# Half of the value copies of a two-layer attention kernel issued from GpSimd's queue instead of SyncE's

## The chip, the cores and the metric

The kernel runs on one core of one Trainium2 chip. The metric is the device time of one execution in microseconds (us); a measurement is the median of several runs. The profile shows one execution, taken by the hardware profiler. In it PE is TensorE (PEld its weight loads), DVE is VectorE, ACT is ScalarE, POOL is GpSimd and SP is SyncE; a "q" behind a name is that engine's instruction queue.

## The reference, cut to what matters

Four residual layers run one after the other over x of 2048 positions by 512 features, bf16: A, B, A, B. Both kinds have 32 heads of 16 features.

```python
def _A_ref(x, wqkv, w_phi, wo):        # linear attention over all positions
    ...
    phi_q = concatenate([softmax(q @ w_phi), softmax(-(q @ w_phi))])   # phi_k likewise
    kv = einsum("bhsf,bhsd->bhfd", phi_k, v);  z = phi_k summed over s
    o = (phi_q @ kv) / (phi_q @ z + 1e-6)
    return o @ wo
def _B_ref(x, wqkv, wo):               # each position sees 8 positions: 0, 2, ..., 14 behind it
    W, dil = 8, 2
    idx = pos[:, None] - (arange(W) * dil)[None, :]
    logits = einsum("bhsd,bhswd->bhsw", q, k[idx]) * Dh ** -0.5     # masked where idx < 0
    return einsum("bhsw,bhswd->bhsd", softmax(logits), v[idx]) @ wo
x = x + _A_ref(_layernorm(x), ...);  x = x + _B_ref(_layernorm(x), ...)
x = x + _A_ref(_layernorm(x), ...);  x = x + _B_ref(_layernorm(x), ...)
```

## The kernel before

The positions are cut into four blocks of 512 (b = 0 to 3); L = 0 or 1 counts the pairs of layers. "Block 12" means L = 1, b = 2. Every piece of work is a step of a named thread, and the string `_ORDER` (lines 57 to 97), written out in full, gives the one order in which all steps are issued. Each engine's queue holds its instructions in that order and runs them strictly one after the other, so an instruction that waits holds up all that stand behind it in the same queue. The buffers are given out by fixed tables (`_SLOTS`); a buffer's next user waits until the last reader is done. A DMA issue waits also for the landing of an earlier DMA that used the same one of eight completion semaphores of its queue.

The steps of a B layer for one block:

- `tr` (line 451, SyncE): a DMA transpose brings the normalised block xn to xnT. It waits for xn.
- `s_b1` (`mm`, line 927, TensorE): the projections to Q, K and V with the weights WB; `ev` copies each result from PSUM (lines 190 and 192, by VectorE or ScalarE). K and V have 16 columns of the block before at their left edge. GpSimd writes these edges with small copies: `halo` for K (line 953), `vhalo_out` (line 969) saves the tail of V and `vhalo_in` (line 965) puts it at the edge of the next block's V.
- `vrep(dl)` (lines 975 to 988), for dl = 0 to 3: four DMAs, one for each g in the order 0, 2, 1, 3, copy 32 rows of V of 4,208 bytes each, shifted by 2g columns, to the partitions 32g to 32g + 31 of a tile Vg. That is 131.5 KB for one DMA, 16 DMAs for a block and 128 for the kernel. "Copies 12.3" below are the four DMAs with dl = 3 of block 12.
- `s_b2` (`prod`, line 1019, VectorE): Q times K at eight shifts, a product of 4096 elements in each partition, four times a block. It reads K's edge. `lgt` (line 1026, TensorE) sums the products to logits, then come exponent, denominator (`den`, line 1042) and the weights PT.
- `s_b3` (`pav`, line 1081, VectorE): PT times Vg, one for each dl; it waits for the four copies of its dl. `mo` (line 1090, TensorE) sums, `ev` copies to oT, and `s_out` (line 520, TensorE, then line 533 on VectorE or 530 on ScalarE) multiplies by WoB and adds the residual.

Where the copies of values stand among the others: before the change all are in SyncE's queue, with the transposes `tr` between them. In `_ORDER` the GpSimd steps and the copies come in this order (tail is `vhalo_out`, V edge is `vhalo_in`, K edge is `halo`):

```
V00 tail | copies 00.0 | V01 edge, K01 edge, V01 tail | copies 01.0 | (tr) | K02 edge, V02 edge |
copies 01.1 01.2 01.3 | (tr, block 03) | copies 00.1 00.2 00.3 02.0 02.1 02.2 | K03 edge, V02 tail, V03 edge |
(tr) | copies 02.3 | (tr) | copies 03.0 03.1 03.2 03.3 | ... layer A ... |
copies 10.0 10.1 | K11 edge | (tr) | V10 tail | copies 10.2 10.3 | V11 edge, K12 edge | (tr) | copies 11.0 |
K13 edge | copies 11.1 11.2 11.3 | V11 tail, V12 edge, V12 tail, V13 edge |
copies 12.0 13.0 13.1 13.2 13.3 12.1 12.2 12.3 | stores of the result
```

The blocks' pavs come in the order 01, 00, 02, 03 in layer 0 and 10, 11, 13, 12 in layer 1; the last pav of blocks 12 and 13 is split in two halves.

Of the kernel before, what the change touches and what calls it, by code (L numbers as in the profile page):

```python
# [30 lines left out]
VGW = 3 * KVW + TB + 8  # L31
# [98 lines left out]
class _Fast:  # L130
# [788 lines left out]
    def s_b1(self, L, b):  # L919
        nc, add = self.nc, self.step  # L920
        st = "b1_%d%d" % (L, b)
        T = {}
        def mm(i, c):
            xnT = self.xnT["B%d" % L, b]
            T[i, c] = pp = self.ps()
            for k in range(NB):
                nc.tensor.matmul(pp[:], lhsT=self.WB[:, k, i * D + c:(i + 1) * D:NB], rhs=xnT[:, :, k, :],  # L927
                                 start=(k == 0), stop=(k == NB - 1))

        def ev(i, c, dve):  # L930
            if i == 0:
                if (L, b) not in self.QT:
                    self.QT[L, b] = self.med([NB, TB], "QT")
                dst = self.QT[L, b][:, c, :]
            elif i == 1:
                ktile()
                dst = self.K[L, b][:, c, 16:KVW]
            else:
                vtile()
                dst = T["V"][:, c, 16:KVW]  # L940
            self.copy(dve, dst, T[i, c][:])

        def ktile():
            if (L, b) not in self.K:
                self.K[L, b] = self.med([NB, KVW], "K")

        def vtile():
            if "V" not in T:
                T["V"] = self.med([NB, KVW], "V")

        def halo():
            ktile()
            nc.gpsimd.tensor_copy(out=self.K[L, b][:, :, 0:16], in_=self.K[L, b - 1][:, :, TB:KVW])

        def kzero():
            ktile()
            nc.gpsimd.memset(self.K[L, b][:, :, 0:16], 0.0)

        def vzero():
            vtile()  # L960
            nc.gpsimd.memset(T["V"][:, :, 0:16], 0.0)

        def vhalo_in():
            vtile()
            nc.gpsimd.tensor_copy(out=T["V"][:, :, 0:16], in_=self.vh[L, b - 1][:])

        def vhalo_out():
            self.vh[L, b] = self.sm([NB, 16], "vh", BF16)
            nc.gpsimd.tensor_copy(out=self.vh[L, b][:], in_=T["V"][:, :, TB:KVW])

        def vwr():
            self.VD[L, b] = self.dram.tile([P, NB * KVW], BF16, name="vd%d%d" % (L, b))
            nc.sync.dma_start(out=self.VD[L, b][:], in_=T["V"][:].rearrange("p c t -> p (c t)"))

        def vrep(dl):
            if dl == 0:
                self.Vg[L, b] = {}
            if dl % 2 == 0:
                self.Vg[L, b][dl // 2] = self.big([2, NB * KVW], "Vg")
            if (L, b) in _OPT["v_dram"]:  # L980
                a = self.VD[L, b][dl:dl + 1, 2:3]
                src = bass.AP(a.tensor, a.offset, [[2, 4], [4 * NB * KVW, H], [1, VGW]])
                nc.sync.dma_start(out=self.Vg[L, b][dl // 2][:, dl % 2, 0:VGW], in_=src)
                return
            for g in (0, 2, 1, 3):
                a = T["V"][dl:dl + 1, 0:1, 2 + 2 * g:3 + 2 * g]
                src = bass.AP(a.tensor, a.offset, [[4 * a.ap[0][0], H], [1, VGW]])
                nc.sync.dma_start(out=self.Vg[L, b][dl // 2][32 * g:32 * g + 32, dl % 2, 0:VGW], in_=src)

        if b:  # L990
            add(st + "v", "POOL", vhalo_in)
        else:
            add(st + "k", "POOL", kzero)
            add(st + "v", "POOL", vzero)
        for i in range(3):
            for c in range(NB):
                add(st + "qkv"[i], "PE", mm, i, c)
                self.flex(st + "qkv"[i], ev, i, c)
        if b:
            add(st + "kh", "POOL", halo)  # L1000
        if b < 3:
            add(st + "v", "POOL", vhalo_out)
        if (L, b) in _OPT["v_dram"]:
            add(st + "v", "SP", vwr)
        for dl in range(4):
            add(st + "v", "SP", vrep, dl)
# [232 lines left out]
class _Layout:  # L1239
# [6 lines left out]
    def add(self, name, nelem, nbuf=1):  # L1246
        self.regions[name] = (self.off, nelem, nbuf)
        self.off += nelem * nbuf
        return self
# [568 lines left out]
```

## Time and profile before

| what | value |
|---|---|
| median of 3 runs | 330.01 us (329.47 to 330.12) |
| span of the profiled execution | 327.5 us, first to last instruction |
| time around the span | 2.5 us, by the median (the profiled execution's own whole time is not recorded) |
| TensorE busy | 310.3 us, 95% |
| VectorE busy | 302.2 us, 92% |
| ScalarE busy | 279.3 us, 85% |
| GpSimd busy | 25.3 us, 8% |
| packets of SyncE's DMA queue | 34.81 MB, 53.6% of the 16 engines' span |
| mean granted TensorE clock | 0.998 |

A busy share is a mean over stages with different limits; the stage tells what a change in it is worth. In a row of a timeline stand the start, the time taken, the engine, the line, the operation, what it writes and reads, the shapes and the count; the brackets give the idle time before it and what ended that. DMA-issuing instructions of SyncE are not counted as busy; a DMA's time "to landing" runs from the start of its issue.

### The profile page before, as it was taken

How to read it: one execution, taken by the hardware profiler on the slowest of the kernel's cores; microseconds unless marked ns; L12 is line 12 of the kernel's file. 1: busy time of each engine (PE TensorE's matmuls, PEld its weight loads, DVE VectorE, ACT ScalarE, POOL GpSimd, SP SyncE). 2: the span in 40 equal slices, each digit the busy share in tenths (PEclk: the TensorE clock that was granted, in tenths of full speed). 3: DMA queues.
4: the chain of work that ended last, by engine and by line, in shares of the span. 5: the costliest groups of instructions: out<-in, count | busy, mean ns of one | idle time of the engine just before them, and what ended most of it. 6: DMA issues, size and time to landing. Idle time of an engine off the chain costs nothing. (4 is left out here: it accounts for less than half of the span.)

```text
span 327.5 us, 8033 instructions
## 1 busy us (share of the span) xinstructions
PE 310.3 (95%) x3176; PEld 149.5 (46%) x3203; DVE 302.2 (92%) x439; ACT 279.3 (85%) x634; POOL 25.3 (8%) x50
## 2 busy tenths in 40 slices
PE   7999999999999999999999999979999999999873
PEld 3655456445444444443444455644544454433221
DVE  7998995998998999899999999699999999999993
ACT  5999988998888999989999999798999996676550
POOL 4000000000021003000000000000000208400000
PEclk9999999999999999999999999999999999999999
DMA  7980000004556899998750300023436977679952
GB/s 197 380 197 3 0 2 4 2 20 120 105 148 135 152 164 133 139 121 154 137 135 1 67 3 2 4 59 90 128 58 125 179 146 134 150 139 158 166 176 92
DMA packets 37388, 35.41 MB, mean 108 GB/s; under 512 B 23008, under 2 KB 32224, under 8 KB 37344
## 3 DMA queue, kind: packets, MB, share of 16 engines
q1 hardware_dynamic: 36816, 34.81, 53.6%
q8 instruction: 27, 0.44, 0.6%
q14 instruction: 17, 0.14, 0.2%
q10 hardware_dynamic: 528, 0.02, 0.1%
HBM read 10.50 MB, written 2.36 MB: 39 GB/s over the span
## 5 line engine op out<-in xcount | busy, mean ns | idle before, releaser
L927 PE MATMUL ps<-xnT,WB 128*128 128x512 bf16 x384 | 87.6, 380 | 0.5 <-DMA xnT<-xn 0.5
L1081 DVE TENSOR_TENSOR pav<-PT,Vg 128x4096 bf16<-128x4096 bf16 (+1 forms) x34 | 72.0, 2162 | 1.5 <-DMA Vg<-V 1.0
L1019 DVE TENSOR_TENSOR prod<-QT,K 128x4096 bf16<-128x4096 bf16 x32 | 72.5, 2291 | 0.3 <-ACT QT L192 0.2
L927 PEld LDWEIGHTS <-WB 128*128 128x128 bf16 x384 | 42.3, 114 | 43.3 <-issue 5.8
L520 PEld LDWEIGHTS <-oT 128*128 128x128 bf16 x256 | 23.8, 97 | 34.5 <-ACT oT L192 5.7
L192 ACT CAST oT<-ps 128x512 bf16<-128x512 f32 (+1 forms) x60 | 32.1, 587 | 8.4 <-PE ps L1090 7.1
L706 ACT ACTIVATE Eq<-ps 128x512 bf16<-128x512 f32 x64 | 34.0, 615 | 0.7 <-PE ps L698 0.6
L520 PE MATMUL ps<-WoB,oT 128*128 128x512 bf16 x122 | 32.1, 380 | 2.4 <-ACT oT L192 2.0
L599 ACT ACTIVATE Ek<-ps 128x512 bf16<-128x512 f32 x64 | 33.6, 622 | 0.4 <-PE ps L593 0.2
L698 PE MATMUL ps<-xnT,WA 128*128 128x512 bf16 x128 | 30.7, 380 | 0.6 <-DVE Eq L816 0.6
L540 ACT ACTIVATE sqd<-x 128x512 bf16<-128x512 bf16 x48 | 30.1, 643 | 1.0 <-DVE x L533 0.8
L605 PE MATMUL ps<-WA,xnT 128*128 128x512 bf16 x120 | 30.0, 380 | 0.5 <-issue 0.2
L593 PE MATMUL ps<-WA,xnT 128*128 128x512 bf16 x124 | 29.7, 380 | 0.6 <-DMA xnT<-xn 0.2
L520 PE MATMUL ps<-WoA,oT 128*128 128x512 bf16 x120 | 29.2, 380 | 0.4
L533 DVE SCALAR_TENSOR_TENSOR x<-ps,x 128x512 bf16<-128x512 f32 x38 | 25.4, 686 | 1.9 <-PE ps L520 1.7
L192 ACT CAST V<-ps 128x512 bf16<-128x512 f32 x31 | 17.5, 595 | 4.4 <-PE ps L927 4.3
L192 ACT CAST K<-ps 128x512 bf16<-128x512 f32 x31 | 17.8, 585 | 3.7 <-PE ps L927 3.3
L530 ACT ACTIVATE x<-ps 128x512 bf16<-128x512 f32 x26 | 15.1, 598 | 6.4 <-PE ps L523 6.3
L192 ACT CAST QT<-ps 128x512 bf16<-128x512 f32 x29 | 17.1, 592 | 2.5 <-PE ps L927 2.5
L651 DVE TENSOR_TENSOR Ek<-Ek,rk 128x4096 bf16<-128x4096 bf16 (+1 forms) x10 | 18.6, 1858 | 0.5 <-ACT rk L646 0.5
L593 PEld LDWEIGHTS <-xnT 128*128 128x128 bf16 x128 | 12.1, 97 | 15.4 <-DMA xnT<-xn 0.7
L446 ACT ACTIVATE xn<-x,nmr,rstd 128x512 bf16<-128x512 bf16 x23 | 18.2, 822 | 1.0 <-DVE nmr L435 0.8
(129 smaller groups left out, 433.3 us busy)
## 6 DMA issues: line engine op xcount, KB each, us to landing
Vg<-V SPq DMA_DIRECT2D x128, 131.5 KB, 4.4
Prho<-rd SPq DMA_DIRECT2D x8, 512.0 KB
x<-in_A_x_dram SPq DMA_DIRECT2D x3, 512.0 KB
WB<-in_B_wqkv_dram SPq DMA_DIRECT2D x3, 512.0 KB, 11.6
wraw<-in_A_wqkv_dram SPq DMA_DIRECT2D x4, 256.0 KB, 4.5
out_dram<-x SPq DMA_DIRECT2D x4, 256.0 KB, 2.2
out_dram<-x SPq DMA_DIRECT2D x8, 128.0 KB, 2.2
x<-in_A_x_dram SPq DMA_DIRECT2D x4, 128.0 KB
```

The costliest lines, as they stand in the source:

```text
L192: self.nc.scalar.copy(out=out, in_=in_)
L520: nc.tensor.matmul(y[:], lhsT=oT[:, c, t * P:(t + 1) * P], rhs=Wo()[:, c, :], start=(c == 0), stop=(c == NB - 1 and not onpe))
L533: nc.vector.scalar_tensor_tensor(out=xb[:, t, :], in0=T[t][:], scalar=1.0, in1=xb[:, t, :], op0=ALU.mult, op1=ALU.add, **kw)
L540: nc.scalar.activation(out=sqd[:], in_=xb[:, t, :], func=ACT.Square, accum_out=T["ss"][:, t:t + 1])
L593: nc.tensor.matmul(pk[:], lhsT=xnT[:, t, k, :], rhs=self.WA[:, k, D:2 * D], start=(k == 0), stop=(k == NB - 1))
L599: nc.scalar.activation(out=T["E"][:, t, s, :], in_=T["k", t][:], func=ACT.Exp, scale=1.0 - 2.0 * s)
L605: nc.tensor.matmul(pv[:], lhsT=xnT[:, t, k, :], rhs=self.WA[:, k, 2 * D:3 * D], start=(k == 0), stop=(k == NB - 1))
L698: nc.tensor.matmul(pq[:], lhsT=self.WA[:, k, hb * P:(hb + 1) * P], rhs=xnT[:, :, k, :], start=(k == 0), stop=(k == NB - 1))
L706: nc.scalar.activation(out=self.Eq[L, b][s][:, :, hb, :], in_=T[hb][:].rearrange("p (t i) -> p t i", t=4), func=ACT.Exp, scale=1.0 - 2.0 * s)
L927: nc.tensor.matmul(pp[:], lhsT=self.WB[:, k, i * D + c:(i + 1) * D:NB], rhs=xnT[:, :, k, :], start=(k == 0), stop=(k == NB - 1))
L1019: nc.vector.tensor_tensor(out=pr[:], in0=QT[:, c:c + 1, :].to_broadcast([P, NW, TB]), in1=win, op=ALU.mult)
L1081: nc.vector.tensor_tensor(out=pv, in0=PT[:, :, lo:lo + n].unsqueeze(1).to_broadcast([P, NB, 2, n]), in1=vw, op=ALU.mult)
```

## The change

In `vrep`, the copies with g = 2 and 3 (partitions 64 to 127 of Vg) are issued from GpSimd's queue, those with g = 0 and 1 still from SyncE's. The order string, the buffers, the sources and destinations stay as they were. Of each `vrep` two DMAs are now on either queue; GpSimd's instructions of the list above stand in one queue with 64 DMA issues.

```diff
             for g in (0, 2, 1, 3):
                 a = T["V"][dl:dl + 1, 0:1, 2 + 2 * g:3 + 2 * g]
                 src = bass.AP(a.tensor, a.offset, [[4 * a.ap[0][0], H], [1, VGW]])
-                nc.sync.dma_start(out=self.Vg[L, b][dl // 2][32 * g:32 * g + 32, dl % 2, 0:VGW], in_=src)
+                q = nc.sync if g < 2 else nc.gpsimd
+                q.dma_start(out=self.Vg[L, b][dl // 2][32 * g:32 * g + 32, dl % 2, 0:VGW], in_=src)
```

## Prediction

> **What bounds the kernel now.** I read the page first, then the stages, the rows of the Vg tiles, and the timelines of SyncE, GpSimd, VectorE and TensorE around the copies.
>
> ```profile
> span 327.5 us, 8033 instructions
> ...
> PE 310.3 (95%) x3176; PEld 149.5 (46%) x3203; DVE 302.2 (92%) x439; ACT 279.3 (85%) x634; POOL 25.3 (8%) x50
> ...
> Vg<-V SPq DMA_DIRECT2D x128, 131.5 KB, 4.4
> ```
>
> The profiled span is 327.5 us; the median of the three runs is 330.0, so 2.5 us lie around the span and I add them to the sum. TensorE and VectorE are both nearly full, SyncE issues all 128 value copies, and GpSimd is idle 92% of the time. By stages (us from the start; busy time of each engine, count, granted clock, share of the DMA engines, GB/s):
>
> ```profile
> core 0: us, PE busy (x) PEld busy (x) DVE busy (x) ACT busy (x) POOL busy (x), PEclk, DMA share, GB/s
> ...
> 122.00:143.00 21.00, 20.84 (x140) 9.22 (x142) 19.83 (x17) 19.14 (x46) 3.04 (x3) 1.00 1.06 137
> 143.00:178.00 35.00, 34.09 (x235) 14.34 (x236) 34.45 (x33) 33.14 (x83) 0.00 (x0) 1.00 0.66 113
> ...
> 247.00:265.00 18.00, 18.00 (x131) 8.65 (x130) 17.22 (x20) 17.40 (x40) 2.65 (x4) 1.00 0.86 150
> 265.00:290.00 25.00, 25.00 (x163) 11.71 (x165) 25.00 (x13) 17.84 (x35) 10.26 (x5) 1.00 0.71 146
> 290.00:308.00 18.00, 15.62 (x134) 5.71 (x128) 18.00 (x11) 12.27 (x28) 0.00 (x0) 1.00 1.06 161
> ```
>
> From 265 to 308 VectorE has not one idle microsecond; what delays it there delays the end. The DMA engines are full (1.06) in two stretches: one copy of 131.5 KB (134,656 bytes) takes 134.7/137 = 0.98 us of them in the first and 134.7/161 = 0.84 us in the second.
>
> ```profile
> L988 SPq DMA_DIRECT2D Vg<-V x128: 467/592/1630, 95.3 to 307.5; - x128
> ...
>   DMA Vg<-V: 1.0, 1
> ...
> DMA to landing us min/median/max: 2.8/4.4/8.5
> ```
>
> SyncE issues one in 0.59 us, faster than the engines carry it (0.84 to 0.98), so issuing is not the limit. In the whole program VectorE waited for a copy once, for 1.0 us:
>
> ```profile
> 135.51 2.29 DVE L1081 TENSOR_TENSOR pav<-PT,Vg 128x4096 bf16<-128x4096 bf16 x1 [1.03 <-DMA Vg<-V]
> ...
> 138.09 2.29 DVE L1019 TENSOR_TENSOR prod<-QT,K 128x4096 bf16<-128x4096 bf16 x1
> ...
> 148.37 0.62 PE L1026 MATMUL ps<-prod,indQK 128*32 128x512 bf16 x8 [0.50 <-DVE prod L1019]
> ```
>
> **Part by part.** Sixty-four copies (g = 2 and 3) leave SyncE's queue for GpSimd's. "Copies 11.2" are those of block L=1, b=1, dl=2: two now on each queue. SyncE loses 64 x 0.59 = 38 us of issuing, worth nothing by itself, for the engines carry what they carried.
>
> *The price of an issue on GpSimd* is not in this trace. One end is SyncE's 0.59 us for the same transfer. The other is a GpSimd instruction held up by VectorE, as its own small copies are: 0.24 us next to instructions that read PSUM, up to 2.30 us next to prod and pav.
>
> ```profile
> 85.60 0.15 POOL L961 MEMSET V<- 128x64 bf16 x1 [41.88 <-PE ps L900]
> ...
> 108.16 0.70 POOL L965 COPY V<-vh 128x64 bf16<-128x64 bf16 x1 [2.72 <-issue]
> ...
> 126.05 0.55 POOL L969 COPY vh<-V 128x64 bf16<-128x64 bf16 x1 [1.69 <-ACT V L192]
> ...
> 249.17 0.24 POOL L953 COPY K<-K 128x64 bf16<-128x64 bf16 x1 [65.42 <-DVE x L533]
> ...
> 270.79 2.24 POOL L953 COPY K<-K 128x64 bf16<-128x64 bf16 x1 [10.27 <-ACT K L192]
> 272.97 2.30 POOL L969 COPY vh<-V 128x64 bf16<-128x64 bf16 x1
> 275.33 2.18 POOL L965 COPY V<-vh 128x64 bf16<-128x64 bf16 x1
> 282.73 1.43 POOL L969 COPY vh<-V 128x64 bf16<-128x64 bf16 x1 [5.22 <-ACT V L192]
> 284.21 2.18 POOL L965 COPY V<-vh 128x64 bf16<-128x64 bf16 x1
> ```
>
> I take 1.1 us, near the geometric mean of 0.59 and 2.30, and a little towards SyncE's row, since that is the same transfer; GpSimd's memset, which reads nothing, took only 0.15. [...]
>
> *The wait at 135.51.* SyncE can't issue copies 00.1 to 00.3 before 119.7, since they stand behind a transpose of xn that waits for ScalarE; they then land too close to their use (SyncE's timeline, and below it TensorE's weight loads).
>
> ```profile
> 105.17 10.45 SPq L988 DMA_DIRECT2D Vg<-V  x12
> 116.73 2.96 SPq L451 DMA_TRANSPOSE xnT<-xn  x1
> 119.73 9.46 SPq L988 DMA_DIRECT2D Vg<-V  x14
> ...
> 122.40 0.55 PEld L927 LDWEIGHTS <-WB 128*128 128x128 bf16 x3
> ```
>
> GpSimd's queue has no transpose in it. After its copy at 108.16, done at 108.9, it issues the twelve of 01.1 to 00.3 back to back: 108.9 + 12 x 1.1 = 122.1. Its halves of 00.1 to 00.3 are thus under way from 108.9 + 6 x 1.1 = 115.5, the SyncE halves (six, not twelve) are issued from 119.7 to 123.5, and the 1.03 us of VectorE's wait go. What is late next is TensorE: it runs 20.84 of 21 us in that stretch and its next wait for VectorE is the 0.50 us at 148.37. So of 1.03 us I credit 0.5.
>
> *The transpose meets the new stream.* It ends its issue at 119.69 and was alone on the engines for 2.4 us:
>
> ```profile
> L451 SPq DMA_TRANSPOSE xnT<-xn x1: 1925/1925/1925, 179.0 to 179.0; - x1
> ...
> DMA to landing us min/median/max: 4.3/4.3/4.3
> ...
> L451 SPq DMA_TRANSPOSE xnT<-xn x1: 2975/2975/2975, 253.3 to 253.3; - x1
> ...
> DMA to landing us min/median/max: 4.6/4.6/4.6
> ```
>
> (The first row is one without copies beside it: 4.3 to landing less 1.9 of issue.) So it lands at 122.1, and TensorE loads weights for block 3 at 122.40. With GpSimd's stream, one copy of 0.98 us of engine time each 1.1 us, beside it until 122.1 and some 0.9 us of its backlog, it gets between all of the engines (no loss) and none until 123 (3.3 us late, less 0.3 of spare time: 3.0). At half: 1.65 of its 2.4 us are done by 123.0, it lands at 123.75, and TensorE starts block 3 some 1.3 us late. The 0.5 us idle at 148.37 absorbs part, and VectorE, relieved of its 1.03 us, no longer makes TensorE wait there. Credit and loss together: +0.8, with -0.5 and +2.5 as ends. I take 0.6, a little below the middle, because of the second row: with copies of 10.1 still in flight (the last was issued at 251.7), that transpose landed 4.6 - 3.0 = 1.6 us after its issue.
>
> *GpSimd's own copies now stand behind DMA issues that wait.* The six issues of 02.0 to 02.2 precede the copy of K03's edge, which was done at 124.4: they start when V02 is complete (the row at 126.05) and end at 126.1 + 6 x 1.1 = 132.7; with its copy, 134.6 at most, against the prod at 138.09 that needs it. Hidden up to 1.6 us an issue. In layer 1 the four issues of 10.0 and 10.1 precede K11's edge:
>
> ```profile
> L988 SPq DMA_DIRECT2D Vg<-V x8: 553/592/594, 247.3 to 251.7; - x8
> ...
> 249.68 2.33 DVE L1019 TENSOR_TENSOR prod<-QT,K 128x4096 bf16<-128x4096 bf16 x1
> ...
> 253.02 2.29 DVE L1019 TENSOR_TENSOR prod<-QT,K 128x4096 bf16<-128x4096 bf16 x1
> ```
>
> 247.3 + 4.4 = 251.7, held by the prod until 252.0, done at 252.3; needed at 253.02. Hidden, with 0.7 to spare: from 1.36 us an issue on, every further 0.1 us costs VectorE 0.4.
>
> *The last stretch.* Now GpSimd's queue is: K13's edge (270.79, done 273.03), six issues of 11.1 to 11.3, four small copies of V edges, then the issues of 12.0, 13.0 to 13.3, 12.1 to 12.3. Before, the last small copy ended at 284.21 + 2.18 = 286.39, and 28 copies of values followed: 28 x 0.84 + 2.8 to landing gives 312.7; the row below has the last but one at 306.6 + 5.7 = 312.3.
>
> ```profile
> L988 SPq DMA_DIRECT2D Vg<-V x1: 468/468/468, 306.6 to 306.6; - x1
> ...
> DMA to landing us min/median/max: 5.7/5.7/5.7
> ...
> 316.21 1.22 DVE L1081 TENSOR_TENSOR pav<-PT,Vg 128x2048 bf16<-128x2048 bf16 x1
> ```
>
> After: 273.03 + 6 x 1.1 = 279.6; four copies at 2.2 beside a full VectorE, 288.5; 30 copies (two of 12.0 wait as well): 288.5 + 25.2 + 2.8 = 316.5, against the pav at 316.21. The 3.5 us of spare time are used up and 0.3 us is lost, one to one. At 0.59 an issue nothing is lost.
>
> *VectorE beside GpSimd's issues.* The prod at 249.68, with GpSimd's small copies beside it, took 2.33 instead of 2.29; the memset has no such trace. 28 issues after 253 cost between 0 and 28 x 0.04 = 1.1; I take 0. The pavs wait for as many landings as before.
>
> Sum: 327.5 + 0.6 + 0.3 = 328.4, with 2.5 around it 330.9. Of this case the own range is 330.0 to 332.2.
>
> **Rivals.** *The relief wins (faster).* If GpSimd issues in 0.85 us or less, its twelve end before 119.2, the transpose finds the engines nearly free, and the last stretch loses nothing. Then the 0.5 us at 148.37, and up to 1.03 if VectorE sets the pace of the stage to 178 (34.45 of 35 us against TensorE's 34.09), come home: 329.0 to 329.5, say 329.3. For it: GpSimd's 8% load. Against: no margin between 122.1 and 122.40.
>
> *Nothing comes through.* Transfers go at the engines' pace whoever issues them, only one wait of 1.0 us was ever for them, and TensorE and VectorE are full elsewhere: gain and loss cancel, 330.0, give or take 0.4. [...] That the copies don't leave SyncE at all can be excluded from the diff.
>
> *GpSimd is slow at issuing.* At 1.5 us: K11's edge 0.5 us late, the six of 11.x end at 282.0, the small copies at 290.9, the last landing at 318.9 against 316.2: +2.7; with the 0.6 of the transpose, 333.8 at most if they add. At 2.3, like a COPY next to prod: 273.03 + 13.8 + 8.9 = 295.7, then 16 issues of 2.3 end at 332.5, 335.3 landed, 19 us late: about 349. It decides from 1.36 on. [...]
>
> **How the numbers follow.** Forecast 0.42, relief 0.20, nothing 0.18, slow issuing 0.20. This kernel's runs differ by 0.65 us, so about 0.2% (0.66 us) is what a measurement can tell. Faster by more: 0.18 of the relief and 0.02 of nothing, 0.20. Slower by more (above 330.67): 0.33 of the forecast and all of slow issuing, 0.53. Within: 0.27. The range 329.2 to 335.0 leaves out the best of the relief (0.05) and the slow issues above 1.6 us (0.12).
>
> **What would show it.** Right: GpSimd shows Vg issues about 1.1 us apart; no DVE idle before the pav of 00.3; a TensorE wait for xnT near 122.5; GpSimd's last small copy ending near 288.5 and the last pavs waiting for Vg by some tenths. Wrong: issues 1.4 us apart or more with VectorE idle before the prod at 253; or no wait for xnT and a span under 327.

## The result and the profile after

The changed kernel took 339.44 us (median of 4 runs, 338.91 to 340.17) beside 329.74 us for the kernel before. The ratio is 1.030, with a 95% interval of 1.028 to 1.032: slower by 9.7 us, where 0.9 had been forecast, and outside the range. The profiled execution has a span of 338.2 us and took 340.17, so 2.0 us lie around its span.

The page of the changed kernel (each engine's busy time; the DMA issues with their median time to landing):

```profile
span 338.2 us, 8082 instructions
...
PE 312.4 (92%) x3176; PEld 149.7 (44%) x3203; DVE 302.8 (90%) x439; ACT 279.4 (83%) x634; POOL 60.3 (18%) x114
...
PEclk9999999999999995999999999999999999999998
...
Vg<-V SPq DMA_DIRECT2D x64, 131.5 KB, 6.1
Vg<-V POOLq DMA_DIRECT2D x64, 131.5 KB, 5.8
```

VectorE's and ScalarE's busy time is that of before to within 0.6 us; there is simply more idle time. The row of granted clocks has a 5 in one slice in the middle, which the page of before did not have. The group of Vg copies shows what an issue costs:

```profile
L989 SPq DMA_DIRECT2D Vg<-V x64: 467/592/1727, 95.3 to 311.9; - x64
L989 POOL DMA_DIRECT2D Vg<-V x64: 529/529/663, 95.7 to 312.0; - x64
```

GpSimd needs 0.53 us for an issue, less than SyncE's 0.59, and never more than 0.66. The stage that had 20.84 us of TensorE work in 21 us now reads (start, end and length, then busy times, clock, DMA share, GB/s):

```profile
122.00:143.00 21.00, 14.56 (x92) 5.66 (x94) 13.87 (x10) 11.67 (x29) 6.35 (x11) 0.84 0.90 131
```

6.3 us of TensorE's work are gone from it, and the mean clock is 0.84. Cut at the points where TensorE stops and starts, after and then before:

```profile
122.70:127.50 4.80, 0.00 (x0) 0.00 (x0) 4.76 (x4) 2.09 (x5) 0.00 (x0) 1.00 1.14 138
127.60:134.30 6.70, 5.22 (x12) 1.62 (x12) 1.92 (x1) 0.58 (x1) 0.00 (x0) 0.50 0.80 97
```

```profile
122.70:127.50 4.80, 4.80 (x46) 2.13 (x46) 4.77 (x4) 4.54 (x11) 2.79 (x3) 1.00 1.02 126
127.60:134.30 6.70, 6.65 (x49) 2.87 (x48) 6.70 (x4) 6.41 (x18) 0.00 (x0) 1.00 1.07 142
```

First nothing runs on TensorE, then twelve matmuls run at half the clock, where before 95 ran. The timelines of SyncE, GpSimd and TensorE, and then of VectorE, tell why:

```profile
103.32 1.70 SPq L451 DMA_TRANSPOSE xnT<-xn  x1
105.06 7.93 SPq L989 DMA_DIRECT2D Vg<-V  x6
116.85 4.69 SPq L451 DMA_TRANSPOSE xnT<-xn  x1
121.59 3.77 SPq L989 DMA_DIRECT2D Vg<-V  x6
```

```profile
108.93 4.33 POOL L989 DMA_DIRECT2D Vg<-V  x8
116.62 2.11 POOL L989 DMA_DIRECT2D Vg<-V  x4 [3.35 <-PE ps L1027]
```

```profile
122.31 0.38 PE L1043 MATMUL ps<-E,indDen 128*128 128x512 bf16 x1
129.07 5.31 PE L927 MATMUL ps<-xnT,WB 128*128 128x512 bf16 x12 [6.39 <-DMA xnT<-xn]
```

In the kernel before, the same twelve matmuls of TensorE read:

```profile
122.61 2.75 PE L927 MATMUL ps<-xnT,WB 128*128 128x512 bf16 x12
```

VectorE after:

```profile
135.86 4.53 DVE L1082 TENSOR_TENSOR pav<-PT,Vg 128x4096 bf16<-128x4096 bf16 x2 [6.34 <-PE ps L1091]
```

Before, twelve copies were carried between the transposes of blocks 02 and 03, and the copies 00.1 to 00.3 stood behind the second in SyncE's queue. Now GpSimd's half of 00.1 to 00.3, six copies, is issued by 118.7, while the engines still carry the copies of 01.1 to 01.3. By the trace's marks of completion all six land before the transpose (the last at 128.52, xnT at 129.03). TensorE waits 6.39 us for xnT, VectorE then 6.34 for TensorE, and the twelve matmuls take 5.31 us where they take 2.75 at full clock: 6.39 + 2.56 = 8.95 us. From there on TensorE's steps stand 8.4 to 9.2 us later than before. VectorE's stand 6.2 to 8.9 us later in the rest of layer 0 and 8.8 to 9.2 in layer 1.

### The profile page after: what moved, and what is told of

Its sections match the earlier page's. It is cut to its first block, busy times and chain, and to the rows that moved or that the text cites. A ratio compares the mean times of both kernels' runs of the same rounds, so it can differ in the third digit from the quotient of the medians.

```text
span 338.2 us, 8082 instructions
## 1 busy us (share of the span) xinstructions
PE 312.4 (92%) x3176; PEld 149.7 (44%) x3203; DVE 302.8 (90%) x439; ACT 279.4 (83%) x634; POOL 60.3 (18%) x114
## 5 line engine op out<-in xcount | busy, mean ns | idle before, releaser
L927 PE MATMUL ps<-xnT,WB 128*128 128x512 bf16 x384 | 90.3, 388 | 7.2 <-DMA xnT<-xn 7.2
L989 POOL DMA_DIRECT2D Vg<-V x64 | 33.9, 532 | 133.6 <-ACT V L192 63.8
```

The source lines that it names most:

```text
L989: q.dma_start(out=self.Vg[L, b][dl // 2][32 * g:32 * g + 32, dl % 2, 0:VGW], in_=src)
```

## The experiments

Two theories stood against each other. *Order:* SyncE's one queue had kept copies behind the transpose; a second queue lets them go first, and each costs about 1 us of DMA time (0.98 by the rows of before). *Meeting:* copies issued by GpSimd slow a transpose whenever they are in flight beside it, however they are ordered. A third question was whether the half clock follows from TensorE's wait, and costs anything. "Before" is the kernel before in the same session, 329.7 to 330.05 us.

**The change with GpSimd's queue held (hold).**

```diff
+            if (L, b) == (0, 0) and dl == 1:
+                hold = self.sm([2], "hold", BF16, 1)
+                nc.gpsimd.tensor_copy(out=hold[:], in_=self.xnT["B0", 3][:, 3, 3, P - 2:P])
             for g in (0, 2, 1, 3):
```

> The whole change, but one tiny GpSimd copy that reads xnT of block 03 stands ahead of the copies 00.1 to 00.3 in GpSimd's queue, so its halves of them can't be issued before that transpose has landed. Order theory (the transpose was late because GpSimd put six more copies in front of it): xnT lands near 122 to 123, TensorE waits for it under 1 us, no stretch at half clock there, the transposes and pavs of the end are back within 1 us of before, and 330 to 331.5 us (up to 1.5 us of the tail may stay). Rival (copies issued by GpSimd slow a transpose, whatever their order): the last transpose and the other copies still meet, and at least 3 us of the loss stay, 333 or more. Clock alone: nothing of its own.

Measured: 332.01 us (331.24 to 334.14), ratio 1.009 (1.006 to 1.013). The stage and VectorE's wait:

```profile
122.70:127.50 4.80, 4.80 (x46) 2.16 (x46) 4.76 (x4) 4.54 (x11) 3.57 (x7) 1.00 1.04 146
127.60:134.30 6.70, 6.64 (x45) 2.84 (x48) 6.54 (x4) 6.42 (x18) 4.46 (x7) 1.00 1.08 160
```

```profile
129.56 4.53 DVE L1085 TENSOR_TENSOR pav<-PT,Vg 128x4096 bf16<-128x4096 bf16 x2 [0.16 <-DMA Vg<-V]
```

The stage is full again at full clock. Of 9.7 us, 7.4 are gone by restoring one order, with all 64 copies still on GpSimd; the median is 2.3 us over before, 0.5 more than the order theory's upper end allows. The profiled execution was the shortest of the six, 331.24.

**Six copies alone (only6), two (only2), four (only4).** All other copies are on SyncE.

```diff
-                q = nc.sync if g < 2 else nc.gpsimd
+                q = nc.gpsimd if g >= 2 and (L, b) == (0, 0) and dl else nc.sync         # only6
+                q = nc.gpsimd if g >= 2 and (L, b) == (0, 0) and dl == 1 else nc.sync    # only2
+                q = nc.gpsimd if g >= 2 and (L, b) == (0, 0) and dl > 1 else nc.sync     # only4
```

> Before, with only six of the copies (the halves g = 2 and 3 of 00.1, 00.2 and 00.3) issued by GpSimd; 122 stay on SyncE. Order theory: these six are the whole loss ahead of the tail, xnT lands near 128 to 129, TensorE waits 6 to 6.5 us for it, then half clock; 337.5 to 339.5 us. Rival (the loss comes from GpSimd's 64 copies in general, each costing a little): a tenth of it, about 331.

> Before, with only the two copies g = 2 and 3 of 00.1 issued by GpSimd (at about 109.5, so they have landed before block 03's transpose is issued at 117). Amount theory (what is ahead of the transpose counts, at 1.0 us of DMA time a copy): xnT lands near 124.1 instead of 122.1, TensorE waits 1.5 to 1.8 us, and the time is 1.2 to 1.6 us over before: 331 to 331.4. Meeting theory (only GpSimd copies in flight beside the transpose delay it): xnT lands near 122.1 to 122.5 and the time is that of before, 329.7.

> Before, with only the four copies g = 2 and 3 of 00.2 and 00.3 issued by GpSimd, near 117 to 119, that is at or after the time at which SyncE begins to issue block 03's transpose (117). First come, first served: at most one of the four is ahead, xnT lands 1 us late and the time is 330 to 331. No order between the two queues: all four are carried before the transpose is done, xnT lands 4 to 7 us late, near 126 to 129, and the time is 334 to 338 with whatever half clock follows.

**The order on SyncE alone (order_sp).** Before, with one step of the order string, block 03's transpose (`9o`), moved behind the copies 00.1 to 00.3 (one `4z` is the four copies of one dl):

```diff
-... 82 9o 82 85 82 50 51 52 4z 4z 4z 9q ...
+... 82 82 85 82 50 51 52 4z 4z 4z 9o 9q ...
```

> Before, all copies on SyncE, but the transpose of block 03 stands behind the copies 00.1 to 00.3 in SyncE's queue. Order theory: the loss comes without GpSimd. The transpose is issued some 7 us later (12 issues of 0.59) behind 24 copies, lands at 129 or later, and the time is 338 to 343 us. Rival (GpSimd's queue is what slows the transpose): it lands 2.4 us after its issue as before, near 129 too only by the issue, and its DMA time from issue to landing stays near 5.4 us; the two are told apart by the issue to landing here: over 8 us by backlog, 5 to 6 by the rival.

Measured, TensorE's timeline at block 03's first twelve matmuls, in the order only2, only4, only6, order_sp:

```profile
124.86 2.78 PE L927 MATMUL ps<-xnT,WB 128*128 128x512 bf16 x12 [1.57 <-DMA xnT<-xn]
```

```profile
127.51 4.17 PE L927 MATMUL ps<-xnT,WB 128*128 128x512 bf16 x12 [4.66 <-DMA xnT<-xn]
```

```profile
131.05 4.07 PE L927 MATMUL ps<-xnT,WB 128*128 128x512 bf16 x12 [8.07 <-DMA xnT<-xn]
```

```profile
134.24 4.29 PE L927 MATMUL ps<-xnT,WB 128*128 128x512 bf16 x12 [10.86 <-DMA xnT<-xn]
```

| kernel | copies put ahead | xnT late, us | TensorE's wait | half clock, us | wait + matmuls over 2.75 | time, us | over before (ratio, 95%) |
|---|---|---|---|---|---|---|---|
| only2 | 2 | 2.0 | 1.57 | none | 1.6 | 331.64 | +1.9 (1.005 to 1.008) |
| only4 | 4 | 5.1 | 4.66 | 3.41 | 6.1 | 336.15 | +6.5 (1.018 to 1.022) |
| the change | 6 | 6.8 | 6.39 | 6.83 | 8.9 | 339.44 | +9.7 (1.028 to 1.032) |
| only6 | 6 | 8.5 | 8.07 | 6.83 | 9.4 | 339.61 | +9.9 (1.029 to 1.033) |
| order_sp | 12, by SyncE | 11.3 | 10.86 | 10.24 | 12.4 | 342.25 | +12.5 (1.035 to 1.041) |

"Late" is the time from the start of the issue of block 02's transpose to the landing of block 03's, less the 18.9 us of before, so that a profile's own start does not enter. What TensorE loses there accounts for the time, to within 0.8 us in every row. Six copies do what 64 do, and the largest loss is the one in which GpSimd issues no copy: it is a matter of order. The test that was to tell the theories apart by order_sp's issue to landing (over 8 us, or 5 to 6) gave 7.35, between them: the time decides it, this number doesn't.

only2's copies had landed (115.1 and 116.0) before the issue of the transpose began (117.45), and it came 2.0 us late, as the amount alone says. only4 asks what "ahead" means (SyncE's and GpSimd's timelines):

```profile
117.01 3.90 SPq L451 DMA_TRANSPOSE xnT<-xn  x1
```

```profile
116.79 2.24 POOL L989 DMA_DIRECT2D Vg<-V  x4 [7.64 <-PE ps L1027]
```

Three of the four issues begin after SyncE began the transpose's, and all four copies landed (121.1 to 126.9) before it: 5.1 us late, not 1. For the landing, first come, first served is out. For the data it is not: by the packet records in the trace, the transpose's 2,048 packets of 256 B start from 119.4 to 122.7, behind one copy, and end 1.3 us later after the start of the issue than before (5.7 for 4.4). The packets of the other three copies follow, from 122.2 to 125.3. The transpose's 4-byte packets, which before start at the end of its data (from 121.0, the last data packet at 121.15), start only at 124.5, and it lands 4.7 us after its last data packet, where before it was 0.9. So the copies issued later held up the landing, not the data. These copies cost 1.28 us each, more than only2's 1.0, so the meeting theory keeps a part. A transpose and the other queue's copies came through together (in the change 71 packets of GpSimd's copies start between the transpose's first and last, 119.9 to 125.6), while on one queue it landed some 2 us after the last copy ahead of it (only2: 122.66 and 124.81) and before the next. only6's transpose came 1.7 us later than in the changed kernel, with the same six copies ahead; why is open.

**Idle matmuls in the wait (fill28: the changed kernel, 28 of them; only6f: only6, 34).** Their result is overwritten.

```diff
             T[i, c] = pp = self.ps()
+            if (L, b) == (0, 3) and not self.filled:
+                self.filled = True
+                for _ in range(28):
+                    nc.tensor.matmul(pp[:], lhsT=self.WB[:, 0, 0:P], rhs=self.WB[:, 0, 0:TB], start=True, stop=True)
```

> The changed kernel with 28 idle matmuls (their result is overwritten) where TensorE would wait for xnT of block 03. They end before xnT lands. Clock theory (the half clock of 127.6 to 134.4 comes from TensorE's idle time): no half clock, the 12 matmuls of block 03 take 2.6 us instead of 5.3, and the time falls by 2 to 3 us to 336.5 to 337.5. Rival (the half clock has another cause, or the time at half clock is hidden by VectorE): 339 to 340.

> The kernel with six copies on GpSimd (339.6 us) with 34 idle matmuls in TensorE's wait for xnT of block 03; no GpSimd copy is in flight later on. Clock theory: no half clock after the wait, the 12 matmuls of block 03 take 2.6 us instead of about 5, and the time falls by 2 to 3 us to 336.6 to 337.6. Rival (other work sets the pace there, the half clock is hidden): 339 to 340.

Measured: fill28 343.14 us (ratio 1.041, 1.038 to 1.045), slower, not faster; only6f 337.77 (336.61 to 338.88), against only6's 339.61. TensorE in fill28, and then in only6f:

```profile
122.66 6.21 PE L930 MATMUL ps<-WB 128*128 128x512 bf16 x28
128.72 2.75 PE L932 MATMUL ps<-xnT,WB 128*128 128x512 bf16 x12
...
271.14 3.54 PE L932 MATMUL ps<-xnT,WB 128*128 128x512 bf16 x8 [4.18 <-DMA xnT<-xn]
```

```profile
123.03 7.50 PE L930 MATMUL ps<-WB 128*128 128x512 bf16 x34
131.13 2.75 PE L932 MATMUL ps<-xnT,WB 128*128 128x512 bf16 x12 [0.60 <-DMA xnT<-xn]
```

In both the clock stays full and the matmuls take 2.75 us. In only6f this brings 1.8 us home, by the medians (its excess over 2.75 was 1.3). In fill28 the matmuls gained their 2.6 us, but then the transpose of block 12 met GpSimd's copies worse than before: 10.7 us to landing, a wait of 4.18 us, and a new half clock of 3.41 us. The forecast for that kernel missed because there is a second place. Its size is not settled by the order of issue: in the changed kernel GpSimd's issues stand as far behind that transpose's (1.2 us), and it landed after 6.7 us.

**Layer 1 alone (l1only).**

```diff
-                q = nc.sync if g < 2 else nc.gpsimd
+                q = nc.gpsimd if g >= 2 and L else nc.sync
```

> GpSimd issues its half of the copies in layer 1 alone (32 of them); layer 0 is as before. Two-site theory: nothing is lost at 122; the transpose of block 12 lands 2 to 3 us late (near 260.5 for 257.9), which costs TensorE 0.6 to 1.0 us, and the end after the last landing takes 2.8 to 3.2 us instead of 2.0: 331 to 332 us. One-site theory (all of the loss is at block 03): 329.4 to 330.2.

Measured: 331.35 us (331.21 to 332.02), ratio 1.005 (1.003 to 1.007). The issue to landing of block 12's transpose (4.6 us before), GpSimd's issues beside it, and TensorE:

```profile
DMA to landing us min/median/max: 7.9/7.9/7.9
```

```profile
255.38 2.11 POOL L989 DMA_DIRECT2D Vg<-V  x4 [2.29 <-PE ps L1027]
```

```profile
262.18 1.89 PE L927 MATMUL ps<-xnT,WB 128*128 128x512 bf16 x8 [1.38 <-DMA xnT<-xn]
```

That transpose was issued at 254.2, ahead of all four copies, and still came 3.3 us late. Its data did not: its last data packet ended 4.1 us after the start of the issue, as before. The landing followed 3.9 us after that, where before it was 0.5. The second place is there; the kernel loses 1.7 us, of which this wait is 1.38. The end after the last landing took 2.2 us, not the 2.8 to 3.2 expected.

**Six copies, held (best6):** the relief of VectorE's wait without the new order, which might have beaten both kernels.

```diff
+            if (L, b) == (0, 0) and dl == 1:        # and the copy that reads xnT, as in hold
...
+                q = nc.gpsimd if g >= 2 and (L, b) == (0, 0) and dl else nc.sync
```

> Before, with only the six copies g = 2 and 3 of 00.1 to 00.3 issued by GpSimd, and these held in its queue by the tiny copy that reads xnT of block 03. Nothing can get ahead of the transpose: it lands near 122 and TensorE does not wait for it. VectorE's wait of 1.0 us before the pav of 00.3 falls to 0.2 or less. Relief theory: 0.4 to 0.9 us of it come home, 328.8 to 329.3 us, a version faster than both. Rival (TensorE sets the pace there, the wait was covered): 329.5 to 329.9, no difference.

Measured: 333.93 us (332.3 to 334.38), ratio 1.011 (1.009 to 1.013): slower by 3.9 us. GpSimd's timeline, VectorE's, TensorE's and the clock (0.57 in the last row is the granted clock):

```profile
122.40 2.13 POOL L987 COPY hold<-xnT 128x2 bf16<-128x2 bf16 x1 [13.31 <-DMA xnT<-xn]
124.47 3.29 POOL L992 DMA_DIRECT2D Vg<-V  x6
```

```profile
131.19 2.29 DVE L1085 TENSOR_TENSOR pav<-PT,Vg 128x4096 bf16<-128x4096 bf16 x1 [1.53 <-DMA Vg<-V]
134.67 2.29 DVE L1085 TENSOR_TENSOR pav<-PT,Vg 128x4096 bf16<-128x4096 bf16 x1 [1.19 <-DMA Vg<-V]
```

```profile
137.01 0.61 PE L1094 MATMUL ps<-pav,indAV 128*32 128x512 bf16 x8 [2.65 <-DVE pav L1085]
137.56 7.06 PE L927 MATMUL ps<-xnT,WB 128*128 128x512 bf16 x24
```

```profile
138.00:142.00 4.00, 4.00 (x12) 1.51 (x11) 3.90 (x4) 1.89 (x6) 0.00 (x0) 0.57 1.07 155
```

The tiny copy, which took 0.35 us in hold, took 2.13 here. VectorE was at a pav in both, and in both the copy ended with that pav (122.1 and 124.5); here the pav had only just begun. GpSimd's halves of 00.1 and 00.2 were issued from 124.5 and came too late: VectorE waited 2.7 us in place of 1.0, TensorE 2.65 us for VectorE, and the clock fell again. Neither theory had this. No version here beats the kernel before.

## Why the prediction was wrong

*The price of an issue on GpSimd* was the first step to fail: 0.53 us, below the lower end of 0.59, not 1.1. Prod and pav don't hold an issue (0.66 at most), while the small copies beside them still take 2.2 us. The rival of slow issuing fell with it.

*The transpose meets the new stream* was the step that cost the forecast: +0.6, with 2.5 as its end, where the runs showed 8.9 at this place. Three things in it were wrong. The backlog of 0.9 us counted GpSimd's stream alone, at 1.1 us an issue, which the engines keep up with; it left out that SyncE's own six copies of 01.1 to 01.3 load the same engines. Even at 1.1 us some ten copies of GpSimd and these six stand ahead at 119.7, and by the rows of before 16 x 0.98 us after 108 is 123.7 for them alone, an estimate. At 0.53 all twelve were out by 118.7. Sharing "at half" was wrong too: all six of GpSimd's copies of 00.1 to 00.3 landed first, and even copies issued later held up the landing, if not the data (4.7 us from the last data packet to the landing in only4, 3.9 in l1only, for 0.9 and 0.5 before). And TensorE did not only lose its wait of 6.39 us: half clock added 2.56.

The rival of the relief took the same price for its condition (0.85 us or less), which was met, and drew the opposite sign from it: "its twelve end before 119.2, the transpose finds the engines nearly free". The end of issuing isn't the end of carrying: the last of GpSimd's six was issued by 118.7 and landed at 128.52. By the rows of before, 18 copies of 0.98 us after 108 and the 2.4 us of the transpose alone gave 128; it landed at 129.0. By this count the faster the issue, the later the transpose.

*Nothing comes through* failed: the DMA work was the same, and no faster (a packet of 4,208 B took 0.39 us in the mean on GpSimd's queue and 0.40 on SyncE's, where before it was 0.38), but its order changed.

*The wait at 135.51* went, as said, in the changed kernel and in hold. Its worth of 0.5 did not come. In hold VectorE's steps stand 0.9 us earlier than before from the pav of 00.3 to 154, and TensorE's wait of 0.50 us at 148.37 is gone. But TensorE then waits 0.80 us for the next transpose, where before it waited 0.20, and VectorE's lead ends in a wait for TensorE (TensorE in hold, then before, and VectorE in hold):

```profile
149.29 1.04 PE L593 MATMUL ps<-WA,xnT 128*128 128x512 bf16 x3 [0.80 <-DMA xnT<-xn]
```

```profile
149.18 1.04 PE L593 MATMUL ps<-WA,xnT 128*128 128x512 bf16 x3 [0.20 <-DMA xnT<-xn]
```

```profile
169.16 0.69 DVE L533 SCALAR_TENSOR_TENSOR x<-ps,x 128x512 bf16<-128x512 f32 x1 [0.76 <-PE ps L520]
```

TensorE was 0.19 us behind before this and 0.11 after it, so under 0.1 us came home; the relief's rival had counted on 0.5 to 1.03.

*GpSimd's own copies* stayed hidden (K11's edge was done at 258.75, its prod came at 261.89), and *the last stretch* lost nothing, as the text said for 0.59 an issue: the last small copy ended at 295.31, 286.1 without the 9.2 of shift, and no pav there waited. What it had not listed is the end: from the last landing 3.2 us to the end of the span, where before it was 1.9; hold had 2.8, only2, only4 and only6, with a few copies on GpSimd, 1.6 to 2.0. SyncE waits there for more completion semaphores (20 waits in the change, 16 before), but l1only has as many and took 2.2; most of the rest is one pause of SyncE between two of these waits (0.9 us in the change, 0.6 in hold), and its cause is open. With the second place at block 12 (0.7 us), the end (0.9) is what the trace of hold still lost. That execution was 1.5 us over before; the 0.8 by which the median lies higher is in no trace.

*Around the span* lay 2.0 us, not 2.5.

## What to carry to other kernels

When DMAs move to another engine's queue, ask first what the old queue kept them behind: a queue is also an order, and the transfer that TensorE needs next may owe its place to nothing else. Transfers issued later on another queue can still hold up its landing (by 3.3 us in l1only). Count a backlog over all queues and in the engines' time for each transfer, not in the time of issuing, above all where the DMA share is already 1 (here 0.98 us to carry a copy and 0.53 or 0.59 to issue it). A wait of TensorE of several us is to be priced with the half clock after it: 1.3 to 2.6 us more here, after waits of 4.66 to 10.86 us.

## What the runs showed of the hardware that was not expected

The half clock came in whole multiples of 3.41 us: 3.41 (only4, fill28), 6.83 (the change, only6), 10.24 (order_sp), after waits of 4.2 (fill28) to 10.9 us, and none after 1.57 (only2) or 1.38 (l1only). In best6 3.41 us of half clock followed a wait of only 2.65 us, and the 3.41 us ahead of that fall held 1.4 us of matmuls, where in the change they held none. The stretches at full clock ahead of the falls were whole multiples too (36 x 3.413 = 122.88 us in the change, only4, only6 and order_sp, 133.12 in best6, 266.24 in fill28), so in these runs the falls stood on one beat of 3.41 us and not at a fixed time after the wait began: 4.9 us after that in the change, with TensorE still idle, and some 4 us after it in best6, 1.4 us after TensorE had started again. What in a wait makes the clock fall is not shown.

On one queue a transpose landed 1.6 to 2.2 us after the last copy ahead of it (before, only2, order_sp). With GpSimd's copies issued 1.2 us after it, block 12's came 2.1 to 6.1 us later than before from issue to landing (the change 6.7, hold 7.1, l1only 7.9, fill28 10.7 us, for 4.6). Most of this lies behind the data: from the last data packet to the landing it was 0.5 us before, and 2.9, 3.2, 3.9 and 5.5 us in these four. The packet records show the transpose's 4-byte packets starting among the packets of those copies (in the change from 266.4 to 267.4, the copies' up to 268.5; before all at the end of the data, 257.38 to 257.43), in fill28 behind nearly all of them. At block 03, where copies were ahead of it, the data came late as well: by all of the 2.0 us in only2 and by 4.4 of the 6.8 in the change. What sets the size of either part is open.
